# Chunked attention feeding a swish layer pair: scores moved one phase further ahead of PV, bank copies on VectorE, and a new order of products and sums

## Chip, cores and metric

The kernel runs on one core of a Trainium2 chip. The metric is the device time of one execution in microseconds (us). Executions of one kernel mostly agree within 1%. Two runs are in the slow state (one of five of e1_sums12, one of four of e10_loads_warm); all others and all profiled ones are in the fast state. Ratios are the mean time of one kernel's fast runs over the mean of the other's in the same rounds on the same chip, so they are not quite the ratio of the medians (of all runs) that are quoted beside them.

PE is the matmul engine (PEld is the loading of its weights, which overlaps it), DVE is VectorE, ACT is ScalarE, POOL is GpSimd, SP is SyncE.

## The reference

```python
# attention inside chunks of 64 tokens: batch 8, heads 8, 576 tokens, head size 64
scores = 0.125 * q_c @ k_c^T ;  attn = softmax(scores) ;  x = attn @ v_c
# x as (4608 tokens, 512), then two layers with a gated unit of width 2048
h = x @ w_in                       # 512 -> 2048
g = h * sigmoid(beta * h)          # silu with a slope for each of the 2048 columns
out = g @ w_out                    # 2048 -> 512
```

## The kernel before

The 4608 tokens are worked in nine blocks of 512, j = 0 to 8. For each block there are scores (PE), their exponentials (ACT), PV (the exponentials times v, PE), a division that also takes the result out of PE's memory (DVE; the "PV eviction"), a transposition by DMA into `xt`, layer 1 (PE, then silu on ACT, giving `g`), and layer 2. Block 0 is plain. In blocks 1 to 8 both layers use a Strassen-Winograd scheme: seven half-size products replace eight, at the price of sums before them and copies of partial results between them. Products collect in "banks" of the memory that PE writes to; one that accumulates on a bank must wait until the bank's last content is copied. Attention for block j+1 is woven into block j.

Half of layer 1 is done by two "units", with plain products ("spacers", `sp(8)` and so on) between their steps:

```python
def unit(j, q, spacers):          # seven products into banks A, B, C
    prod("A", a11, b11, True)
    snap("u1", "A", "a")          # copy of bank A on ACT
    spacers[0]()
    prod("A", swr[1], ts[1], False)      # accumulates on A: must wait for the copy u1
    snap("u2", "A", "v")                 # copies on DVE
    prod("C", swr[0], ts[0], True)
    snap("w1", "C", "v")
    spacers[1]()
    prod("A", swr[2], ts[2], False)
    snap("u3", "A", "v")
    nc.gpsimd.tensor_tensor(out=sb["t"], in0=sb["u3"], in1=sb["w1"], op=ALU.add)   # POOL
    prod("B", a12, b21, True)            # the "upward half" product
    nc.vector.tensor_tensor(out=c1[:, :, up_], in0=bank["B"], in1=sb["u1"], op=ALU.add)
    spacers[2]()
    prod("A", a22, ts[3], False); prod("C", swr[3], b22, False)
    nc.vector.tensor_tensor(out=c1[:, :, dn_], in0=bank["C"], in1=sb["u2"], op=ALU.add)
    # six silus on ACT: of t, of bank A, of c1
```

`ts` are four DVE differences of the block's input (`emit_xs`). Layer 2 needs four sets of sums of `g`, in four parts each (`emit_sum(j, which, part)`): s1, s2 and s4 on DVE, s3 on POOL; s2 needs s1, and s4 needs s2. Layer 2's products on bank A are, in order, `mm[0]` (g), `mm[2]` (s2), `mm[4]` (s3), `mm[6]` (s1). `mm[1]` and `mm[3]` are the products B and D, and `mm[5]` is C, which reads s4. `cB`, `cD`, `cC` are DVE additions of a bank and a copy. The order of a block was:

```python
L1(j, ...)      # emit_xs(j); unit 0; sp(11); unit 1; sp(15); dve(4): four of the eight s1/s2 sums
                # then the first score group of block j+1 (emit_sc)
mm[0]()
while fill: dve()                     # the other four s1/s2 sums
mm[1](); cB()
go(at); go(at)                        # PV 0 of block j+1, second score group
emit_sum(j, 4, 0); emit_sum(j, 4, 1)
mm[2](); go(tr); go(at)               # tr: DVE transposes of q/k; at: PV 1
emit_sum(j, 4, 2); emit_sum(j, 4, 3)
mm[3](); go(at); go(tr)               # PV 2
mm[4](); cD(); go(at); go(tr)         # PV 3
mm[5](); cC(); go(tr)
mm[6]()
load_v(j + 2); load_qk(j + 3)         # DMA issues on POOL's queue
```

The engines work strictly in the order written here. No scheduler reorders.

The softmax here doesn't subtract the row's maximum and nothing guards it: scores larger than these inputs give would overflow.

## Time and profile before

| | before |
|---|---|
| time, first three runs, median | 333.89 us |
| profiled span | 332.2 us |
| PE busy | 278.7 us (84%) |
| DVE / ACT / POOL busy | 67% / 51% / 42% |
| mean granted clock | 0.974 |

The first listing is the windows view of the kernel before, for layer 2 of block 4 and layer 1 of block 5. The columns are the stretch, its length, the busy time of each engine (and instructions), then PE's granted clock, the DMA share and GB/s.

```profile
core 0: us, PE busy (x) PEld busy (x) DVE busy (x) ACT busy (x) POOL busy (x), PEclk, DMA share, GB/s
183.44:197.41 13.97, 13.97 (x238) 11.79 (x238) 13.12 (x22) 5.63 (x9) 3.95 (x3) 1.00 0.28 68
197.41:218.41 21.00, 16.34 (x157) 9.81 (x155) 11.35 (x21) 13.19 (x24) 10.89 (x11) 0.92 0.86 116
```

Layer 2 is dense: PE is busy for all of its 13.97 us. DVE is nearly full as well, at 13.12 us. Layer 1 takes 21.0 us for 16.3 us of PE work, so the loose time is there.

The second listing is the chain of waits of the kernel before in layer 1 of block 4: start, length, what.

```profile
164.67 1.27 POOL o L463
165.94 3.38 POOL vb L98 x4
...
170.70 1.34 POOL t L329
...
174.92 0.58 ACT gt L254
175.50 0.48 ACT u L306
...
176.02 0.60 PE wA L297 x4
```

The chain runs through POOL's load issues to POOL's addition `t`, then the silus, then the copy `u1` on ACT. This copy stands behind the silus of unit 0, and PE waits for it. The waits view of the kernel before (who waited for whom: total us, times, longest) has the sum over the run, 16.6 us:

```profile
PE wA L297 <- ACT u L306: 16.6, 8, 2.6
```

The last listing of the kernel before is PE's timeline in the second half of layer 2, block 4: start, length, group, and idle time before it in brackets.

```profile
189.70 1.92 PE L398 MATMUL oD<-tw,gt 128*128 128x256 f16 x16
...
191.80 1.92 PE L398 MATMUL oA<-tw,s 128*128 128x256 f16 x16
...
193.91 1.92 PE L398 MATMUL oC<-w_out,s 128*128 128x256 f16 x16
```

There are no brackets: PE waits for nothing here, and each product takes 1.92 us from its first matmul to its last (they start some 1.75 us apart when they follow each other).

### The profile page before, as it was taken

The page shows a single profiled execution, that of the slowest core. Times are in us where ns is not written, and L with a number is a line of the kernel's source. Part 1 is how long each engine was busy: PE and PEld are TensorE (multiplying, and loading weights), DVE is VectorE, ACT ScalarE, POOL GpSimd, SP SyncE. Part 2 cuts the span into 40 slices and gives each one's busy share as a digit, 9 for nine tenths or more (in the row PEclk, how much of TensorE's full clock was granted, in tenths as well). Part 3 has the DMA queues.
Part 4 walks back from the last instruction along what each step waited for, and adds up shares of the span by engine and source line. Part 5 has one row for each costly group of instructions (what it writes and reads, how often), then busy time and mean ns, then how long its engine had stood idle before and what let it go on. Part 6 is the DMA issues. An engine that isn't in the chain of part 4 may idle for free.

```text
span 332.2 us, 8211 instructions
## 1 busy us (share of the span) xinstructions
PE 278.7 (84%) x3520; PEld 191.1 (58%) x3520; DVE 222.5 (67%) x377; ACT 170.8 (51%) x288; POOL 139.9 (42%) x130
## 2 busy tenths in 40 slices
PE   2889976688986998699797988799879987998785
PEld 0464432356854686458654875478547854775475
DVE  3653668859992699359855985399748564856573
ACT  1278056068246744646166626581667166716630
POOL 8622499344065315623374327431743134312430
PEclk9999999599999899989999999799999999999999
DMA  7999999400379034912494239514901410151012
GB/s 115 173 207 212 185 205 222 105 1 2 81 139 181 9 65 129 176 38 51 85 182 91 51 89 166 102 33 89 143 3 34 98 63 0 35 97 64 1 34 95
DMA packets 69588, 31.99 MB, mean 96 GB/s; under 512 B 53680, under 2 KB 63920, under 8 KB 69552
## 3 DMA queue, kind: packets, MB, share of 16 engines
q0 software_dynamic: 44960, 18.35, 45.1%
q1 hardware_dynamic: 24448, 12.99, 15.1%
q8 instruction: 27, 0.44, 0.6%
q10 hardware_dynamic: 144, 0.13, 0.1%
q14 instruction: 9, 0.07, 0.1%
HBM read 36.71 MB, written 9.44 MB: 139 GB/s over the span
## 4 chain that ended last, share of the span: by engine, by line
PE 40%; ACT 15%; DMA 14%; POOL 14%; DVE 10%; issue 5%; POOLq 0%; DVEq 0%
PE oA L398 14%; ACT gt L311 11%; DMA w_out<-in_moe_w_out_dram 10%; POOL t L329 5%; PE hps L244 5%; PE oD L398 4%; PE oB L398 4%; PE wA L297 4%; POOL vb L98 4%; DMA ku<-in_k_dram 2%; PE wX L297 2%; DMA xt<-x 2%; DVE u L308 2%; PE x L186 2%; DVE xs L277 2%
## 5 line engine op out<-in xcount | busy, mean ns | idle before, releaser
L244 PE MATMUL hps<-xt,wi 128*128 128x512 f16 (+1 forms) x336 | 83.7, 380 | 6.3 <-DMA xt<-x 5.2
L254 ACT ACTIVATE gt<-hps,beta 128x512 f16<-128x512 f32 x80 | 54.2, 687 | 46.1 <-PE hps L244 46.0
L362 POOL TENSOR_TENSOR s<-gt 128x512 f16<-128x512 f16 x32 | 39.5, 1254 | 47.6 <-ACT gt L311 47.6
L244 PEld LDWEIGHTS <-wi 128*128 128x128 f16 x336 | 33.0, 100 | 32.6 <-DMA xt<-x 7.2
L308 DVE COPY u<-wA 128x512 f32<-128x512 f32 x32 | 22.1, 691 | 43.5 <-PE wA L297 42.8
L398 PEld LDWEIGHTS <-s 128*128 128x128 f16 x496 | 46.8, 98 | 6.0
L297 PEld LDWEIGHTS <-sw 128*128 128x128 f16 x256 | 25.9, 104 | 42.2 <-issue 20.9
L398 PE MATMUL oA<-tw,s 128*128 128x256 f16 x368 | 44.1, 273 | 0.0
L297 PE MATMUL wA<-xs,sw 128*128 128x256 f16 x128 | 21.5, 295 | 26.8 <-ACT u L306 16.6
L398 PEld LDWEIGHTS <-gt 128*128 128x128 f16 x384 | 35.8, 98 | 9.2 <-ACT gt L311 4.6
L329 POOL TENSOR_TENSOR t<-u,w 128x512 f32<-128x512 f32 x16 | 20.6, 1286 | 34.9 <-DVE u L308 34.9
L443 POOL TENSOR_TENSOR w<-u,u 128x512 f32<-128x512 f32 x7 | 8.9, 1270 | 58.5 <-ACT u L409 58.5
L409 ACT COPY u<-oA 128x512 f32<-128x512 f32 x24 | 14.1, 588 | 37.5 <-PE oA L398 37.5
L98 POOL DMA_DIRECT2D vb<-in_v_dram x32 | 27.5, 876 | 8.6 <-DMA wi<-in_moe_w_in_dram 4.8
L167 ACT ACTIVATE et<-sc 128x512 f16<-128x512 f32 x34 | 18.5, 594 | 18.0 <-PE sc L158 17.9
L203 DVE TENSOR_TENSOR x<-x,rd 128x512 f16<-128x512 f32 x34 | 23.5, 692 | 1.3
L130 DVE STREAM_TRANSPOSE qT<-qu 128x576 f32<-128x576 f32 x16 | 20.0, 1250 | 6.1 <-DMA qu<-in_q_dram 6.1
L158 PE MATMUL sc<-qT,kT 32*64 32x64 f16 x1088 | 14.2, 195 | 11.7 <-DVE kT L130 6.5
L297 PEld LDWEIGHTS <-wi 128*128 128x128 f16 x192 | 19.1, 100 | 8.0 <-issue 0.4
L358 DVE TENSOR_TENSOR s<-gt 128x512 f16<-128x512 f16 x32 | 21.0, 657 | 3.7 <-ACT gt L311 3.7
L158 PEld LDWEIGHTS <-kT 32*64 32x64 f16 x1152 | 12.2, 111 | 18.1 <-issue 8.9
L130 DVE STREAM_TRANSPOSE kT<-ku 128x576 f32<-128x576 f32 x16 | 19.9, 1243 | 2.1 <-DMA ku<-in_k_dram 2.1
(81 smaller groups left out, 437.5 us busy)
## 6 DMA issues: line engine op xcount, KB each, us to landing
out_dram<-osb SPq DMA_DIRECT2D x21, 256.0 KB, 3.1
vb<-in_v_dram POOLq DMA_DIRECT2D x32, 144.0 KB, 5.2
qu<-in_q_dram POOLq DMA_DIRECT2D x7, 576.0 KB, 7.8
ku<-in_k_dram POOLq DMA_DIRECT2D x7, 576.0 KB, 9.9
out_dram<-o SPq DMA_DIRECT2D x14, 256.0 KB, 2.2
wi<-in_moe_w_in_dram POOLq DMA_DIRECT2D x4, 512.0 KB, 12.7
w_out<-in_moe_w_out_dram POOLq DMA_DIRECT2D x4, 512.0 KB, 16.8
qu<-in_q_dram POOLq DMA_DIRECT2D x2, 288.0 KB, 5.5
```

The source lines that it names most:

```text
L98: nc.gpsimd.dma_start(out=t[64 * hp:64 * hp + 64, 2 * z:2 * z + 2, :, 0:D].rearrange("p s c d -> p (s c) d"), in_=v[b, h0:h0 + 2].rearrang ...
L130: nc.vector.transpose(out=dst[b][:, z].rearrange("p t r e -> p (t r e)").bitcast(FP32).rearrange("p (t r) -> p r t", r=RUN), in_=src[b][:, ...
L158: nc.tensor.matmul(out=sc[a % 2][o0:o0 + 64, z, c, :], lhsT=kk[:, cb * CH:(cb + 1) * CH, e], rhs=qq[:, cb * CH:(cb + 1) * CH, e], start=(e ...
L203: nc.vector.tensor_tensor(out=yy, in0=src, in1=rr.to_broadcast(shape), op=ALU.mult,)
L244: nc.tensor.matmul(out=hps_t[j, m][:, c0:c1], lhsT=w_r[m // 4][:, 2 * z + e, m // 2 % 2, m % 2, :], rhs=xt_t[j][:, n, c0:c1], start=(n == ...
L254: nc.scalar.activation(out=gt_t[j][:, m, :], in_=hps, func=ACTF.Silu, scale=beta2[:, m % 2, m // 2:m // 2 + 1],)
L297: nc.tensor.matmul(out=bank[b][:, i, :], lhsT=a[:, kk, q, i, :], rhs=rhs[:, kk, :], start=(first and i == 0 and kk == 0), stop=(kk == 1), ...
L308: nc.vector.tensor_copy(out=sb[nm], in_=bank[b])
L311: nc.scalar.activation(out=gt_t[j][:, m, cols], in_=src, func=ACTF.Silu, scale=beta2[:, m % 2, m // 2:m // 2 + 1],)
L329: nc.gpsimd.tensor_tensor(out=sb["t"], in0=sb["u3"], in1=sb["w1"], op=ALU.add)
L362: tt(out=s3[:, lo], in0=g[:, lo, up], in1=g[:, lo, dn], op=ALU.subtract)
L398: nc.tensor.matmul(out=bank[name][:, i, :], lhsT=a[:, kk, i * 128:(i + 1) * 128], rhs=b[:, kk, :], start=(first and i == 0 and kk == 0), s ...
```

## The change

The intent is to shorten layer 1. All bank copies of the unit go to DVE, and the upward half product comes second, so that PE has work while the first copy is made. PV of the next block moves up by one or two products, so that `xt` and its differences are ready when layer 1 starts; for that, scores are made one phase earlier. In layer 2 the s3 product goes second on A, so that the DVE sums get more time.

```diff
 def unit(j, q, spacers):
     prod("A", a11, b11, True)
-    snap("u1", "A", "a")
+    snap("u1", "A")                       # DVE
+    prod("B", a12, b21, True)
+    nc.vector.tensor_tensor(out=c1[:, :, up_], in0=bank["B"], in1=sb["u1"], op=ALU.add)
     spacers[0]()
...                                        # prod B and its addition removed further down
 def mm2():
-    prod("A", s_(2), t2, False)
+    prod("A", s_(3), t3, False)
 def mm4():
-    prod("A", s_(3), t3, False)
+    prod("A", s_(2), t2, False)
...                                        # w1 follows: u1 - u2 instead of u2 - u3
 # L1: emit_xs(j) leaves its head, the dve(4) at its end is removed
 # the block, for j > 1:
 L1(j, ...)                                # with two q/k transposes on DVE, one inside unit 1 and one after it
 mm[0](); pv(0); go(tr)
 mm[1](); cB(); pv(1); go(tr)
 mm[2](); pv(2)
 dve(4)                                    # first four s1/s2 sums
 mm[3](); pv(3)
 while fill: dve()                         # other four
 sc(0)                                     # scores of block j+2
 mm[4](); cD()
 emit_sum(j, 4, 0) ... emit_sum(j, 4, 3)   # s4, all four parts
 mm[5](); cC(); sc(1)
 emit_xs(j + 1)
 mm[6]()
 load_qk(j + 3); load_v(j + 2)
```

(Cut: block 1, which needs three score groups, and the last block's variant of `mm5`.)

More of the change, by code (lines that the diff above doesn't have):

```diff
@@ L301, in prod, with snap @@
                     )
-        def snap(nm, b, eng):
+        def snap(nm, b):
             sb[nm] = u_p.tile([128, 2, HT], FP32, tag=nm, name=nm)
-            if eng == "a":
-                nc.scalar.copy(out=sb[nm], in_=bank[b])
-            else:
-                nc.vector.tensor_copy(out=sb[nm], in_=bank[b])
+            nc.vector.tensor_copy(out=sb[nm], in_=bank[b])
         def silu(m, cols, src):
@@ L318, in unit @@
         prod("A", a11, b11, True)
-        snap("u1", "A", "a")
+        snap("u1", "A")
+        prod("B", a12, b21, True)
+        nc.vector.tensor_tensor(out=c1[:, :, up_], in0=bank["B"], in1=sb["u1"], op=ALU.add)
         spacers[0]()
         prod("A", swr[1], ts[1], False)
-        snap("u2", "A", "v")
+        snap("u2", "A")
         prod("C", swr[0], ts[0], True)
-        snap("w1", "C", "v")
+        snap("w1", "C")
         spacers[1]()
         prod("A", swr[2], ts[2], False)
-        snap("u3", "A", "v")
+        snap("u3", "A")
         sb["t"] = u_p.tile([128, 2, HT], FP32, tag="t", name="t")
         nc.gpsimd.tensor_tensor(out=sb["t"], in0=sb["u3"], in1=sb["w1"], op=ALU.add)
-        prod("B", a12, b21, True)
-        nc.vector.tensor_tensor(out=c1[:, :, up_], in0=bank["B"], in1=sb["u1"], op=ALU.add)
         spacers[2]()
@@ L430, in mm2 @@
         def mm2():
-            prod("A", s_(2), t2, False)
+            prod("A", s_(3), t3, False)
             take("u2", "A")
+            if last:
+                return
+            sb["w1"] = u_p.tile([128, 2, HM], FP32, tag="w1", name="w1")
+            nc.gpsimd.tensor_tensor(out=sb["w1"], in0=sb["u1"], in1=sb["u2"], op=ALU.subtract)
         def mm3():
@@ L437, in mm4 @@
         def mm4():
-            prod("A", s_(3), t3, False)
+            prod("A", s_(2), t2, False)
             take("u3", "A")
             if last:
-                return
-            sb["w1"] = u_p.tile([128, 2, HM], FP32, tag="w1", name="w1")
-            nc.gpsimd.tensor_tensor(out=sb["w1"], in0=sb["u2"], in1=sb["u3"], op=ALU.subtract)
+                sb["w1"] = u_p.tile([128, 2, HM], FP32, tag="w1", name="w1")
+                nc.vector.tensor_tensor(out=sb["w1"], in0=sb["u1"], in1=sb["u2"], op=ALU.subtract)
+                nc.vector.tensor_tensor(out=sb["w1"], in0=sb["w1"], in1=sb["u3"], op=ALU.add)
         def mm5():
@@ L449, in mm5 @@
             prod("E", s_(1), t1, True)
-            for r, other in ((1, "u3"), (0, "u2")):
+            for r, other in ((1, "u3"), (0, "w1")):
                 if r:
@@ L543, in L1 @@
             first()
-        emit_xs(j)
         unit(j, 0, [sp(8), sp(9), sp(10)])
@@ L554, in L1 @@
             fill.extend([lambda w=w, p=p: emit_sum(j, w, p) for w in (1, 2)])
-        dve(4)
         hooks.get(KFF, lambda: None)()
@@ L638, with pv, sc @@
             hooks = {}
-            if na < NB:
-                hooks[KFF] = lambda: emit_sc(2 * na)
+            tr = T_items(j + 2) if j + 2 < B else []
             if j == 1:
                 T2 = T_items(2)
-                hooks.update({9: T2[0], 11: T2[1], 13: T2[2], 15: T2[3]})
-            L1(j, hooks, (lambda: emit_xp(7)) if j == 1 else None)
-            at = []
-            if na < NB:
-                at = [
-                    lambda: emit_pv(4 * na), lambda: emit_sc(2 * na + 1),
-                    lambda: emit_pv(4 * na + 1), lambda: emit_pv(4 * na + 2),
-                    lambda: emit_pv(4 * na + 3),
-                ]
-            tr = T_items(j + 2) if j + 2 < B else []
+                hooks = {9: T2[0], 11: T2[1], 13: T2[2], 15: T2[3], KFF: lambda: emit_sc(4)}
+                emit_xp(7)
+                emit_xs(1)
+            elif tr:
+                hooks = {13: tr.pop(0), 15: tr.pop(0)}
+            L1(j, hooks)
+            def pv(n):
+                if na < NB:
+                    emit_pv(4 * na + n)
+            def sc(n):
+                if na + 1 < NB:
+                    emit_sc(2 * na + 2 + n)
             def go(lst):
@@ L659 @@
             mm[0]()
+            if j > 1:
+                pv(0)
+            go(tr)
+            mm[1]()
+            cB()
+            if j == 1:
+                pv(0)
+                emit_sc(5)
+            else:
+                pv(1)
+            go(tr)
+            mm[2]()
+            if j == 1:
+                pv(1)
+            else:
+                pv(2)
+            dve(4)
+            go(tr)
+            mm[3]()
+            if j == 1:
+                pv(2)
+            else:
+                pv(3)
             while fill:
                 dve()
-            mm[1]()
-            cB()
-            go(at)
-            go(at)
-            emit_sum(j, 4, 0)
-            emit_sum(j, 4, 1)
-            mm[2]()
-            go(tr)
-            go(at)
-            emit_sum(j, 4, 2)
-            emit_sum(j, 4, 3)
-            mm[3]()
-            go(at)
+            if j > 1:
+                sc(0)
             go(tr)
@@ L677 @@
             cD()
-            go(at)
-            go(tr)
+            emit_sum(j, 4, 0)
+            emit_sum(j, 4, 1)
+            if j == 1:
+                pv(3)
+                sc(0)
+            emit_sum(j, 4, 2)
+            emit_sum(j, 4, 3)
             mm[5]()
@@ L682 @@
                 cC()
-            go(tr)
+            if j > 1:
+                sc(1)
+            if na < NB:
+                emit_xs(na)
             mm[6]()
+            if j == 1:
+                sc(1)
+            if j + 3 < B:
+                load_qk(j + 3)
             if j + 2 < B:
                 load_v(j + 2)
-            if j + 3 < B:
-                load_qk(j + 3)
 _INS = ['q', 'k', 'v', 'moe_w_in', 'moe_w_out', 'moe_beta']
```

## The prediction

> **What bounds it now.** The windows view splits a steady block (j = 2 to 8) into two phases. Layer 2 (seven products of 1.75 us) takes 14.2 us with PE 100% and DVE 13.3 us busy. Layer 1 takes 18.6 to 21.1 us with PE only 14.2 to 16.6 busy, so the loose time lies there. The chain of waits says why: output copy (ACT 0.6), its POOL add (1.27), V and q/k load issues (POOL 3.4 + 1.4), POOL `t` add (1.3), silus (2.9), POOL third-sum pair (2.27) and, in parallel, ACT's late copy `u1` of unit 1 (PE idle 1.9 to 2.6 us before it), `t` again, silus, first layer-2 product. The 2.0 us wait for the transposed input at the block's start is mostly hidden behind POOL's loads in blocks 2 to 5. In blocks 2, 3 and 5 the 2.6 us gap is followed by about 3 us at a granted clock of 0.50. The Trainium skill ("TensorE: Matmul & The Clock Gate", Part 1) gives half rate after about a 3.4 us idle window; this trace shows it after a shorter gap.
>
> **What the change moves.** No product is added or removed. `u1` goes to DVE (0.69 us), the upward half product fills its wait, scores leave the layer 1/2 seam, PV starts one to two products earlier, so the input and its sums are ready when layer 1 starts. But DVE's order in layer 2 changes: eight layer-2 sums that ran partly during layer 1's silu tail now stand behind three PV evictions (0.9 each) and two transposes (1.1 each); the fourth sums stand behind the D combination, directly before the product that reads them.
>
> **Costs, laid out from traced durations (estimates).**
> Layer 1: blocks 2 to 5 remain bound by POOL: 6.8 us to `t`, 1.3, silus 2.9, sums 2.3, `t` 1.3, silus 2.9 = 17.5 us, against 19.4 to 21.1: -12 us in all. Blocks 6 to 8: about 16 against 18.7: -8. Block 1: -1.5.
> Layer 2: DVE owes about 9.6 us of work between 1.95 us after the start and the last second-sum part, which is ready at 11.5 us; PE wants it from 8.5: stall about 2.4 us in the product of s2 (now third on A). Then copy 0.6 + combination 0.65 + first fourth-sum 0.4 and latencies: about 1.9 us stall before C. One more score group (0.65) stands inside. Layer 2 becomes about 19 us: +5 in blocks 2 to 5, +4 in 6 and 7, +7 in block 1 (three score groups, an exp wait), +2 at the tail, in total +37.
> The PE, done early with layer 1, idles 3 to 4 us for the silus before layer 2, so half clock moves into the first products there: about +5 net.
> Sum: 334 - 21.5 + 37 + 5 = about 353 us.
>
> **Predicted:** 353 us, 80% range 342 to 363. Faster by over 2%: 0.06; within 2%: 0.08; slower by over 2%: 0.86.
>
> **What would show it.** Right: layer 1 spans of 16 to 18 us with no wait on ACT's `u1`; PE gaps of 2 us or more on A waiting for DVE's second sum and of 1.5 to 2 us before C on DVE's fourth sum; layer 2 spans of 18 to 20 us; clock 0.5 at its start. Wrong: layer 2 near 15 us with no DVE wait on PE, or layer 1 unchanged because a transpose waits for the q load ahead of `u3`.
>
> **What would make it wrong.** If DVE's sums run while PE still waits for the silus (order says not), the stalls vanish and the layer 1 gain would give about 315. If the clock drops more often, over 360.

## The result, and the profile after

| | before | after |
|---|---|---|
| time, median of 4 runs | 333.66 us | 372.43 us |
| ratio of fast runs | | 1.1164 (95%: 1.1118 to 1.121) |
| profiled span | 332.2 us | 370.5 us |
| PE busy | 278.7 us | 297.1 us |
| mean granted clock | 0.974 | 0.917 |

The change made the kernel 11.6% slower. The number of matmuls is the same, 3520, yet PE's busy time grew by 18.4 us. That is a first hint that the matmuls themselves ran slower.

The next table splits the spans by stage. Layer 1 is taken from the start of the block's first unit product to the end of the last silu of `c1`, and layer 2 from there to the next block's first unit product. All numbers are read from the timelines, in us.

| | before | after | difference |
|---|---|---|---|
| start to end of layer 1 of block 1 | 79.47 | 78.90 | -0.6 |
| layer 1, blocks 2 to 8 | 21.0, 21.3, 19.6, 20.9, 18.8, 18.8, 18.8 | 16.2, 17.6, 17.6, 17.6, 16.2, 15.7, 15.7 | -22.5 in all |
| layer 2, blocks 1 to 7 | 14.0 each | 24.9, 21.1, 23.2, 23.2, 23.1, 21.6, 20.9 | +59.9 in all |
| layer 2 of block 8 and tail | 15.5 | 17.0 | +1.5 |

Layer 1 got what was hoped for, and layer 2 lost nearly three times as much. Here is the windows view of the changed kernel for the same two stages, layer 2 of block 4 and layer 1 of block 5:

```profile
199.66:222.77 23.11, 19.14 (x301) 13.64 (x302) 14.02 (x29) 5.73 (x9) 3.53 (x3) 0.78 0.19 48
222.77:240.45 17.68, 13.93 (x93) 8.78 (x91) 10.27 (x14) 11.89 (x22) 10.87 (x11) 1.00 1.02 130
```

Layer 2 went from 13.97 to 23.11 us. PE is idle there for 4 us, and the granted clock is 0.78 where it was 1.00. DVE has about as much to do as before, 14.02 against 13.12 us. PE's timeline of the changed kernel in this stretch shows where:

```profile
199.05 0.28 PE L395 MATMUL oA<-w_out,gt 128*128 128x256 f16 x1 [2.97 <-ACT gt L308]
199.66 2.76 PE L395 MATMUL oA<-w_out,gt 128*128 128x256 f16 x13 [0.33 <-ACT gt L308]
...
209.93 0.39 PE L395 MATMUL oA<-tw,s 128*128 128x256 f16 x2
212.33 0.61 PE L395 MATMUL oA<-tw,s 128*128 128x256 f16 x4 [2.00 <-DVE s L357]
213.12 1.94 PE L395 MATMUL oA<-tw,s 128*128 128x256 f16 x10 [0.18 <-DVE s L357]
216.85 3.59 PE L395 MATMUL oC<-w_out,s 128*128 128x256 f16 x16 [1.79 <-DVE s L361]
```

The third product on A stops for 2.00 us after two matmuls, until DVE has the second part of s2. Product C starts 1.79 us late, for the first part of s4. And C takes 3.59 us where it took 1.92. The waits view has the sums over the run. Only matmul rows are shown here; ACT's copy, which held PE for 16.6 us before, is no longer in the list.

```profile
PE oA L395 <- DVE s L357: 17.2, 15, 3.1
...
PE oC L395 <- DVE s L361: 12.3, 8, 1.8
```

The windows view of the changed kernel, one us at a time, says why:

```profile
212.00:213.00 1.00, 0.61 (x4) 0.31 (x4) 0.97 (x3) 0.60 (x2) 0.00 (x0) 1.00 0.30 61
213.00:214.00 1.00, 0.88 (x6) 0.71 (x7) 0.06 (x1) 0.00 (x0) 0.00 (x0) 0.77 0.35 70
214.00:215.00 1.00, 1.00 (x5) 0.45 (x3) 0.00 (x0) 0.00 (x0) 0.00 (x0) 0.50 0.00 0
...
219.00:220.00 1.00, 1.00 (x6) 0.69 (x5) 0.00 (x0) 0.00 (x0) 0.00 (x0) 0.50 0.00 0
220.00:221.00 1.00, 1.00 (x67) 0.60 (x64) 0.45 (x1) 0.00 (x0) 0.00 (x0) 0.81 0.00 0
```

From about 213.6 to 220.4 us the granted clock is one half. The trace's clock record has one or two stretches of 3.41 or 6.83 us at one half in every layer 2 from block 1 to block 7. In the kernel before it has none in layer 2 until the tail, and from block 2 on three of 3.41 us in layer 1 (blocks 2, 3 and 5). Finally the DVE part of the chain of waits of the changed kernel, which is what PE waited for:

```profile
207.76 0.69 DVE x L203
208.45 0.94 DVE s L355
...
210.79 0.69 DVE x L203
211.48 0.34 DVE s L355
...
215.15 0.59 ACT u L406
...
215.77 0.69 DVE osb L414
216.46 0.34 DVE s L361
...
216.85 3.59 PE oC L395 x16
```

The sums (L355 and L357, s1 and s2) start only after the third PV eviction (`x`), and are cut by the fourth. The s4 sums (L361) stand behind the addition `osb` (`cD`), which itself waits for the copy `u` on ACT of a product that has just ended.

Layer 1 after the change waits no more for ACT's copy, and its blocks 3 to 5 take 17.6 us, as predicted. POOL's loads still stand in it, as the timeline of the changed kernel in layer 1 of block 4 shows: `t` starts when the last load is issued, and the silus wait for `t`.

```profile
185.53 3.43 POOL L98 DMA_DIRECT2D vb<-in_v_dram  x4
...
188.92 1.33 POOL L328 TENSOR_TENSOR t<-u,w 128x512 f32<-128x512 f32 x1
...
190.29 0.91 ACT L308 ACTIVATE gt<-t,beta 128x256 f16<-128x256 f32 x2 [2.66 <-POOL t L328]
```

### The profile page after: what moved, and what is told of

Read it like the earlier page. It is cut to its first block, busy times and chain, and to the rows that moved or that the text cites. A ratio compares the mean times of both kernels' runs of the same rounds, so it can differ in the third digit from the quotient of the medians.

```text
span 370.5 us, 8247 instructions
## 1 busy us (share of the span) xinstructions
PE 297.1 (80%) x3520; PEld 196.3 (53%) x3520; DVE 221.0 (60%) x395; ACT 159.9 (43%) x270; POOL 136.6 (37%) x130
## 4 chain that ended last, share of the span: by engine, by line
PE 46%; DVE 23%; DMA 10%; ACT 10%; POOL 5%; issue 4%; DVEq 0%; ACTq 0%; POOLq 0%
PE oA L395 14%; DMA w_out<-in_moe_w_out_dram 9%; PE hps L244 8%; ACT gt L308 8%; PE oC L395 6%; PE wA L297 6%; PE oB L395 4%; DVE x L203 4%; PE wX L297 4%; DVE s L355 4%; DVE s L357 2%; DVE osb L414 2%; POOL s L359 2%; POOL t L328 2%; DMA ku<-in_k_dram 2%
## 5 line engine op out<-in xcount | busy, mean ns | idle before, releaser
L395 PEld LDWEIGHTS <-s 128*128 128x128 f16 x496 | 50.5, 110 | 49.9 <-DVE s L357 21.3
L395 PE MATMUL oA<-tw,s 128*128 128x256 f16 x368 | 51.5, 293 | 17.2 <-DVE s L357 17.2
L395 PEld LDWEIGHTS <-gt 128*128 128x128 f16 x384 | 38.4, 105 | 29.6 <-ACT gt L308 21.3
L359 POOL TENSOR_TENSOR s<-gt 128x512 f16<-128x512 f16 x32 | 36.2, 1154 | 47.4 <-ACT gt L308 47.4
L464 POOL TENSOR_TENSOR o<-t,o 128x512 f32<-128x512 f32 x7 | 8.9, 1270 | 100.7 <-ACT o L461 100.7
L305 DVE COPY u<-wA 128x512 f32<-128x512 f32 x48 | 33.1, 689 | 18.7 <-PE wA L297 18.7
L395 PE MATMUL oA<-w_out,gt 128*128 128x256 f16 x128 | 21.6, 314 | 17.7 <-ACT gt L308 17.6
L395 PE MATMUL oC<-w_out,s 128*128 128x256 f16 x112 | 23.6, 391 | 12.3 <-DVE s L361 12.3
L201 DVE RECIPROCAL rd<-x 128x8 f32<-128x8 f32 x34 | 6.7, 196 | 34.2 <-PE x L186 34.2
L203 DVE TENSOR_TENSOR x<-x,rd 128x512 f16<-128x512 f32 x34 | 23.5, 691 | 1.3
L308 ACT ACTIVATE gt<-t,beta 128x256 f16<-128x256 f32 x32 | 14.5, 500 | 19.8 <-POOL t L328 19.6
```

Of the source, the lines that this page charges most:

```text
L203: nc.vector.tensor_tensor(out=yy, in0=src, in1=rr.to_broadcast(shape), op=ALU.mult,)
L305: nc.vector.tensor_copy(out=sb[nm], in_=bank[b])
L308: nc.scalar.activation(out=gt_t[j][:, m, cols], in_=src, func=ACTF.Silu, scale=beta2[:, m % 2, m // 2:m // 2 + 1],)
L359: tt(out=s3[:, lo], in0=g[:, lo, up], in1=g[:, lo, dn], op=ALU.subtract)
L395: nc.tensor.matmul(out=bank[name][:, i, :], lhsT=a[:, kk, i * 128:(i + 1) * 128], rhs=b[:, kk, :], start=(first and i == 0 and kk == 0), s ...
```

## The experiments

The theory: the loss is the place of the DVE sums, which makes PE wait twice per block, and these waits halve the clock. The rival: the earlier scores and PV make layer 2 long by themselves. The first four kernels ran together (before: 332.36 us). The changed kernel was not run again with them, so differences to it compare across rounds, between which the kernel before differs by 1.3 us.

### e1_sums12: only the s1/s2 sums back to their places

```diff
 # end of L1
+dve(4)
 mm[0]()
+while fill: dve()
 pv(0) ...
 mm[2](); pv(2)
-dve(4)
 mm[3](); pv(3)
-while fill: dve()
```

> Only the eight first and second sums of layer 2 go back to where they stood before (four at the end of layer 1, four after the first product). Theory (DVE's order makes PE wait, and the waits halve the clock): the 2.0 us gap inside the third product on A goes, the 1.8 us gap before C stays, still followed by half clock in C; about 3 us a block less in seven blocks, 345 to 353 us. Rival (the second score group and the earlier PV make layer 2 long by themselves): 367 us or more.

Measured: 351.24 us, ratio to before 1.0576 (1.054 to 1.0612). The gap in the third product is gone, and the wait before C is still there (15.0 us over the run). This is as the theory said, but for one thing: half clock was expected after each wait before C, and it follows in blocks 2 and 4 only, though the wait is 1.8 to 2.4 us long in all of blocks 2 to 7.

### e2_sums4: only the s4 sums moved, ahead of the third product on A

```diff
+for p in range(4): emit_sum(j, 4, p)
 mm[4](); cD()
-emit_sum(j, 4, 0) ... emit_sum(j, 4, 3)
 mm[5]()
```

> Only the four fourth sums move, ahead of the third product on A and so ahead of the D combination. Theory: the 1.8 us gap before C goes and C runs at full clock (1.75 us, not 3.5); the 2.0 us gap in the third product stays; about 3.5 us a block less, 344 to 352 us. Rival: 367 us or more.

Measured: 351.54 us, ratio 1.0594 (1.0552 to 1.0635). The wait before C is gone from the waits view, and the one in the third product stays (17.2 us). That wait of 2.0 us, now alone, is followed by half clock in blocks 6 and 7 and not in blocks 2 to 5. Each of the two placements costs about 20 us.

### e3_both: both moves of the sums

> Both moves of the sums together, all else as in the changed kernel. Theory: no PE gap on DVE's sums over 0.8 us, layer 2 takes 15.5 to 17 us (first product still partly at half clock after the silu wait), layer 1 stays at 15.8 to 17.7: 324 to 333 us, so no worse than the kernel before. Rival: layer 2 stays over 19 us and the time over 350 us.

Measured: 326.28 us, ratio 0.9813 (0.9787 to 0.984). This is 46 us below the changed kernel, about the sum of the two single moves (21 each), and 1.9% faster than the kernel before (the interval lies on both sides of 2%). Layer 1 stays at 15.7 to 17.6 us, and layer 2 is 16.2 to 16.8 us in blocks 1 to 6. The rival falls: with all else moved, layer 2 is 2 to 3 us longer than before in these blocks (some half clock at its start included), not 7 to 11. PE's timeline of this kernel, around the third product on A of block 3:

```profile
156.53 0.71 PE L158 MATMUL sc<-qT,kT 32*64 32x64 f16 x64
157.17 1.92 PE L395 MATMUL oA<-tw,s 128*128 128x256 f16 x16
158.93 1.91 PE L395 MATMUL oC<-w_out,s 128*128 128x256 f16 x16
```

No brackets are left. The early place is not free: POOL's s3 sums run at the same time. The timeline of e3_both at the start of the same layer 2:

```profile
146.87 0.43 DVE L355 TENSOR_TENSOR s<-gt 128x512 f16<-128x512 f16 x1 [0.90 <-ACT gt L308]
146.92 2.68 POOL L359 TENSOR_TENSOR s<-gt 128x512 f16<-128x512 f16 x2 [2.96 <-ACT gt L308]
147.33 1.26 DVE L357 TENSOR_TENSOR s<-s,gt 128x512 f16<-128x512 f16 x1
148.51 1.37 DVE L355 TENSOR_TENSOR s<-gt 128x512 f16<-128x512 f16 x1
```

Beside POOL's pair the same DVE sum takes 1.26 and 1.37 us instead of 0.43. The Trainium skill ("SBUF — State Buffer", section "Who interferes with whom") says that a DVE instruction with two SBUF inputs contends with a POOL instruction that reads SBUF, and that the later one blocks. This trace agrees. In the changed kernel, where the sums came later, seven of the eight in a block run at 0.41 to 0.43 us. That saves some 1.2 us of DVE time (1.26 + 1.37 - 2 x 0.43, less the 0.6 that one late sum still lost), but waiting for the later slot cost far more.

### e4_warm: the changed kernel, its gaps filled with matmuls of zeros

```diff
+emit_idle(10 if 3 <= j <= 5 else 5 ...)   # before mm[0], 128x512 matmuls of zeros
 mm[0]() ...
+more_idle(warm_t, 10)                      # before the third product on A
 mm[4]()
+more_idle(warm_t, 8)                       # before C
 cD() ...
```

(The count before `mm[0]` is 10 in blocks 3 to 5 and 5 elsewhere.)

> The changed kernel with 8 to 10 extra 128x512 matmuls of zeros into a spare bank in each of the three gaps of layer 2 (nothing waits for them; they only fill the gaps). Theory: the waits on DVE stay as long, but the granted clock stays 1.0 in layer 2, C takes 1.75 us, and the part of the loss that is clock comes back: 3 to 4 us a block, 345 to 352 us. If the clock costs little: 366 us or more. If the filling delays the products: over 373 us.

Measured: 354.47 us, ratio 1.0674 (1.0644 to 1.0703): 2.5 us above the range that the theory gave, but 18 us below the changed kernel. The results are correct, and nothing reads what the extra matmuls write. PE's timeline of e4_warm around product C of block 4:

```profile
204.44 1.27 PE L400 MATMUL oA<-tw,s 128*128 128x256 f16 x10 [0.18 <-DVE s L362]
205.54 1.89 PE L233 MATMUL idle<-zero 128*128 128x512 f16 x8
207.50 2.27 PE L400 MATMUL oC<-w_out,s 128*128 128x256 f16 x16
```

C takes 2.27 us instead of 3.59, and the last ten matmuls on A take 1.27 instead of 1.94. The clock record has no half-speed stretch from layer 2 of block 1 on until the tail. Layer 2 of blocks 1 to 7 now takes 23.5, 19.6, 19.6, 19.6, 19.6, 19.6 and 18.9 us. So of the 59.9 us that layer 2 lost, 17.7 were clock (layer 2 of the changed kernel less that of e4_warm, summed over blocks 1 to 7), and 42.2 were waiting and added work at full clock. The filling may itself add a few tenths of a us in a block, so the clock's part is, if anything, a little more.

The next four kernels (before: 332.73 us) ask which part of the change shortened layer 1.

### e5_copies: the kernel before with the unit's new order alone

The edit is the `unit` part of the change put into the kernel before: the copy `u1` on DVE and product B second.

> The kernel before with one part of the change alone: in layer 1 the first bank copy on VectorE and the upward half product second. Theory (layer 1 of the kernel before was held by ACT's late copy in front of unit 1, and this part alone removes it): layer 1 falls to 17.6 to 18 us in blocks 2 to 5 and 17 to 17.5 in 6 to 8, layer 2 stays 14.0: 312 to 320 us, faster than both kernels. Rival (layer 1 got shorter because scores and PV moved ahead and the input is there early): 328 us or more.

Measured: 334.75 us, ratio 1.0055 (0.999 to 1.0119). The expectation missed by 15 us. Layer 1 takes 18.6 to 21.0 us in blocks 2 to 8, no better than before. PE's timeline of e5_copies at the start of block 4's layer 1 shows the new wait:

```profile
160.60 0.60 PE L297 MATMUL wA<-xt,wi 128*128 128x256 f16 x4
161.04 0.60 PE L297 MATMUL wX<-xt,wi 128*128 128x256 f16 x4
163.21 1.04 PE L244 MATMUL hps<-xt,wi 128*128 128x512 f16 x4 [1.57 <-DMA xt<-x]
165.50 1.01 PE L297 MATMUL wA<-xs,sw 128*128 128x256 f16 x4 [1.25 <-DVE u L305]
```

The copy is now in DVE's queue, behind the four differences of `emit_xs`, and these wait for the transposed input. So the copy that ACT used to make at once waits for the input too. Half clock comes on top: in this block the matmul groups after the gaps take 1.01 us in place of 0.60, and the clock record has a stretch of 3.41 us at one half in each of blocks 3 to 8. In blocks 3 to 5 there are two gaps near each other, in blocks 6 to 8 a single one of 2.16 to 2.17 us; the single gap of 2.22 us in block 2 has none.

### e6_scores: e3_both with the old unit

> e3_both with the layer 1 unit of the kernel before (ACT's copy, upward half product late): scores and PV ahead, without the copies part. Theory: PE waits again for ACT's copy, 2 to 3 us in each block, layer 1 of 18 to 20 us: 338 to 347 us. Rival: layer 1 stays at 16 to 18 us and the time within 2 us of e3_both's.

Measured: 346.35 us, ratio 1.0389 (1.0324 to 1.0454). PE waits 23.1 us over the run for ACT's copy, and layer 1 is 17.1 to 21.2 us. Over blocks 2 to 8 that is 2.2 us less than before, while layer 2 of blocks 1 to 7 is 14.4 us longer; the loss of 13.6 us stands there. So neither part alone shortens layer 1 by much: by 2.2 us with early input alone, not at all with the DVE copy alone, and by some 21 us with both (e3_both).

### e7_swap: the kernel before with the s3 product second

> The kernel before with only the third sum's product second on A instead of third. Theory: POOL's third sums are ready 1.4 us before the product that now reads them, so nothing waits: within 2 us of the kernel before, 331 to 335 us (two more DVE additions at the tail). If POOL's sums come late: over 337 us.

Measured: 332.85 us, ratio 0.9982 (0.9916 to 1.0047). This part of the change has no effect by itself that the runs can tell from none.

### e8_warm0: e3_both with zeros before the first product of layer 2

```diff
+emit_idle(10 if 3 <= j <= 5 else 5)
 mm[0]()
```

> e3_both with 5 to 10 matmuls of zeros in the gap before the first product of layer 2, where its half clock comes from. Theory: clock 1.0 in layer 2, its first two products at 1.6 and 1.75 us instead of 2.2 and 2.8; about 1 us a block less: 318 to 323 us. If DVE (the PV evictions behind the contended sums) already set layer 2's pace: 325 to 327.

Measured: 324.95 us, ratio 0.9759 (0.9707 to 0.981), the best ratio, though its interval overlaps that of e3_both. The clock stays at 1.0 through the steady part, yet layer 2 falls only from 16.3 to 16.0 us: at full clock PE waits for the PV evictions of DVE (6.1 us over the run, 1.3 in e3_both), which stand behind DVE's early sums in the order written. The second expectation, 325 to 327 us, was the nearer one.

The last three (before: 332.23 us) went after layer 1's next limit, POOL.

### e9_loads, e10_loads_warm, e11_before_loads: POOL's load issues moved into layer 2

```diff
 mm[2]()                       # e9 and e10, on e3_both; e11: after mm[3] of the kernel before
+load_qk(j + 3); load_v(j + 2)
 ...
 mm[6]()
-load_qk(j + 3); load_v(j + 2)
```

e10 has five matmuls of zeros before `mm[0]` on top.

> e3_both with the V and q/k load issues moved from the end of a block to after layer 2's third product, where POOL is idle for over 7 us. Theory (layer 1 of 17.6 us in blocks 3 to 5 is held by POOL, whose load issues stand before its first addition t): layer 1 falls to 15.7 to 16.2 in blocks 3 to 5 and 15.7 in block 6, layer 2 unchanged: about 1.8 us a block in four blocks less, 316 to 321 us. Rival (the silus or DVE set layer 1): within 2 us of e3_both, 324 to 328.

> e9_loads with five matmuls of zeros before the first product of layer 2. With the gap there down to about 1.6 us they fill most of it: clock 1.0, 0 to 2 us faster than e9_loads: 315 to 320 us. If the gap no longer halves the clock in e9_loads, equal to it.

> The kernel before with the load issues moved into layer 2 (after its fourth product). Theory: in the kernel before, POOL's loads and the wait for the transposed input end within 0.2 us of each other, and ACT's late copy stands behind both, so moving the loads alone gives little: 329 to 334 us. Rival (POOL's loads, which the chain of waits names, hold it): 1.5 us or more a block less in four blocks, 327 us or below.

Measured: e9 354.12 us, ratio 1.0645 (1.0603 to 1.0687); e10 349.62 us, ratio 1.0482 (1.0401 to 1.0562); e11 360.53 us, ratio 1.0819 (1.075 to 1.0889). All three expectations failed, by 27 to 33 us above their ranges. The DMA part of the pages shows it: first e3_both, then e9_loads (issuing queue, count, size, median us from issue to landing).

```profile
xt<-x SPq DMA_TRANSPOSE x28, 2.6
```

```profile
xt<-x SPq DMA_TRANSPOSE x28, 8.3
```

The transposition of the block's input now shares the DMA engines with 1.7 MB of loads and lands 5.7 us later. Layer 1 of blocks 2 to 5 grew to 22.6 to 24.0 us, with PE waiting for `xt`. In these kernels the end of the block, after the last transposition had landed, was the better place for the loads. The theory that POOL's issues hold layer 1 at 17.6 us is therefore not tested by these runs. What supports it is only the traces: block 6, with 3.4 us of loads, takes 16.2, and blocks 7 and 8, with none, take 15.7.

## Why the prediction was right or wrong

The direction, the mechanism and the places were right; the size was not. The prediction said 353 us with a range to 363 (its terms add up to 354.5), and the kernel takes 372.

- **Layer 1: right.** Predicted -21.5 us in all, measured -23.1 (-22.5 and -0.6). Blocks 2 to 5 were predicted at 17.5; blocks 3 to 5 took 17.6, block 2 took 16.2.
- **PE waits on DVE's sums: right in place and length.** Predicted 2.4 us before s2's product and 1.9 before C; the trace shows 2.00 + 0.18 and 1.79. e1_sums12 and e2_sums4 take away one each, and e3_both takes away both with the whole loss.
- **Layer 2 at full clock: a little low.** Predicted +37 us with the tail. With the clock held up by e4_warm it is +42.2, and +1.5 at the tail. Blocks 2 to 6 took 5.6 us more, where 4 to 5 had been counted, and block 1 took 9.4, where 7 had been counted. This is 6.7 us of the miss.
- **The clock: the step that failed.** The prediction put it as "half clock moves into the first products there: about +5 net". It is 17.7 us (layer 2 of the changed kernel less that of e4_warm). The term was mis-sized because half clock was counted only for the silu wait ahead of layer 2, not for the two waits that the prediction itself had found inside layer 2. Each is only about 2 us long, and the prediction took them for pure waiting. In the trace they are met by 6.83 us at clock 0.50 in blocks 3 to 7, and with that the end of the third product and nearly all of C ran at half speed. The timelines of the two kernels split the 17.7 us: 6.5 lie before the end of product D in blocks 2 to 5, after the silu wait, not far from the +5; 9.8 lie behind product D in blocks 3 to 7, after the two waits; and 1.5 in block 1. The prediction had even noted that in the kernel before a 2.6 us gap was enough, and had named the risk ("If the clock drops more often, over 360").
- Together: -23.1 + 43.7 + 17.7 = +38.3 us, the measured difference of the spans.

The Trainium skill ("TensorE: Matmul & The Clock Gate", section "HAM oscillation — how this bites in real kernels") gives the rule that no gap should exceed about 3.4 us. For this kernel it is too mild: a gap of 2.0 us was enough in blocks 3 to 7. But in block 2 gaps of 1.99 and 1.73 us were not. What the page says of a free-running window of about 3.4 us (Part 1, section "What's actually happening") fits the records: in all 13 traces the changes of the clock lie whole multiples of 3.41 us apart.

Where a gap falls between these marks tells the cases apart. Cut the 13 traces at the marks, from 60 us on. Of the pieces at full clock, 894 were followed by full clock, and in each of them PE was busy for 46% or more; 61 were followed by half clock, and in 60 of them PE was busy for 45% or less (the exception, with 56%, is in block 1 of the changed kernel). Four such pieces of the changed kernel, in the windows view, with the columns as before:

```profile
131.63:135.04 3.41, 1.88 (x14) 1.21 (x14) 1.84 (x5) 1.60 (x4) 0.00 (x0) 1.00 0.19 38
135.04:138.46 3.42, 1.87 (x14) 1.13 (x15) 2.03 (x5) 0.44 (x1) 0.00 (x0) 1.00 0.23 77
...
210.14:213.55 3.41, 1.23 (x10) 0.71 (x9) 2.79 (x8) 2.37 (x3) 0.00 (x0) 1.00 0.26 53
213.55:216.96 3.41, 1.62 (x9) 0.88 (x8) 1.19 (x3) 0.59 (x1) 0.00 (x0) 0.50 0.00 0
```

The first two are block 2: marks cut its two gaps, PE is busy for 55% of each piece, and the clock stays full. The last two are block 4: its first gap lies whole within one piece (36% busy), and half clock follows; the gap before C falls into the next piece, and half clock goes on for one more. So part of the clock's loss is a matter of chance: the same gaps, placed otherwise between the marks, brought no half clock in block 2.

One more reading fell in the experiments. The prediction called the 2.0 us wait for the input "mostly hidden", and e5_copies was expected to gain from the DVE copy alone. But the copy moved into a queue that waits for that same input.

## What to carry to other kernels

When work is moved between stages, write down each engine's new order and ask of every product when its last operand is made: sums that ran in another engine's shadow held nobody there, and made PE wait in their new place. Count each new PE gap near 2 us as a wait, and as a risk of 3.4 us or more at half clock after it. Whether that comes depends on where the gap falls, so widen the range by it; filling the gap with matmuls of zeros tells the two apart. Before moving a DMA issue to an idle queue slot, look which transfers it will share the DMA engines with, not only at the engine that issues it.

## What the Trainium skill lacked or had wrong

- "TensorE: Matmul & The Clock Gate": the rule of gaps over about 3.4 us is too mild here. Gaps of 2.00 and 1.79 us in one stretch of layer 2 went with 6.83 us at clock 0.50 (block 4), gaps of 1.99 and 1.73 us with none after them (block 2), and e5_copies shows 1.57 and 1.25 us with 3.41 us at one half. Single gaps of 1.6 us before layer 2 did not halve it in blocks 7 and 8 and did in block 2.
- The same page has no figure for how busy PE must be for the clock to stay up. In these 13 traces the line lies between 45% and 46% of a piece of 3.41 us, with one exception in 955.
- The same page's sections on the clock gate do not say that matmuls of zeros which nobody reads keep the clock up: e4_warm has no half-speed stretch between layer 2 of block 1 and the tail, at 18 us less than the same kernel without them.
- "DMA: Bandwidth & Descriptors": it tells how queues share an engine packet by packet, but has no figure for a DMA transposition beside loads from POOL's queue. Here the median landing went from 2.6 to 8.3 us (e3_both, e9_loads).
